# Linear attention in front of two expert layers: key/value sums, numerators and denominators issued in five bursts per unit instead of in each step

## The chip, the cores and the metric

The kernel runs on one core of a Trainium2 chip. The metric is the device time of one execution in microseconds, the median over three runs. Inputs and outputs lie in device memory; the clock runs from the first instruction to the last, with the launch around it.

## The reference

Only the first third of the reference, linear attention, is touched by the change. Per batch and head (8 x 8, 576 tokens, head size 64):

```python
def phi(x):                                # 64 -> 128 -> 256 features
    proj = np.einsum('bhsd,df->bhsf', x, w_phi)
    proj = proj - np.max(np.abs(proj), axis=-1, keepdims=True)
    return np.concatenate([np.exp(proj), np.exp(-proj)], axis=-1)
q_p, k_p = (phi(q), phi(k))
kv = np.einsum('bhsf,bhsd->bhfd', k_p, v)
z = np.sum(k_p, axis=2)
num = np.einsum('bhsf,bhfd->bhsd', q_p, kv)
den = np.einsum('bhsf,bhf->bhs', q_p, z)[..., None] + 1e-06
out = num / den
```

Its output goes through a top-1 mixture of 8 experts (512 -> 1024 -> 512) and then through a dense layer with a softmax gate, a norm and a second matrix. Those two layers, the last two thirds of the time, are not edited.

## The kernel before, in words

**Units and steps.** Attention is cut into 8 units: a pair of batches (`p2`) by a group of four heads (`g`). A unit is 9 key jobs k0 to k8 and 9 query jobs q0 to q8. Jobs 0 to 3 belong to the first batch of the pair (half 0), 5 to 8 to the second (half 1), and job 4 holds the last 64 tokens of both. The main loop (L682) runs over 72 steps `st`, one k and one q job each; in the last unit the keys come first.

One step issues, in this order on TensorE (PE), which executes the order as written:

- `s0` for the *next* step (L255): four 128-wide transposes of loaded k and q, which ScalarE (ACT) and VectorE (DVE) split into `hi` and `lo`;
- twice: `proj` (L267 to L269), six matmuls against `w_phi` into a PSUM tile `mm` (four buffers). DVE then takes a maximum (L271) and subtracts it (L273); ACT exponentiates keys into `e` (L277, L278). Behind each `proj` come `q_features` (L330) of the job two steps back, and some small finishing pieces ("f" items: transposes L399, L416, L545, L560);
- `accum_kv` (L283) for the key job of two steps back. It is eight matmul instructions on 64 columns of the array (two instructions run side by side), called here a kv series; jobs 4 and 5 have a series that uses only 64 rows as well (called rest). GpSimd (POOL) adds the same `e` into `es` (L322, L298), which later gives z;
- up to two "64" items: numerators, `num_part` (L440), on 64 columns like kv;
- up to one "32" item: `z_sum` (L384) or `den_part` (L454), on 32 columns, four instructions side by side.

So the array is used in three widths in each step: 128, then 64, then 32 columns. Below, "step i" is the step whose kv series belongs to key job k_i, which is `st` = 9 x unit + i + 2.

`finish_kv` (L468) makes the items of a half after job 4 or job 8: one `z_sum` that may run from the next step, four `num_part` (two token ranges `CHUNKS` of 256 and 320 columns by two head pairs) and two `den_part`, each behind the pieces that it needs (`kf_part` for numerators, `z_part` behind `z_sum` for denominators). When all are done the finishing chain starts (division on DVE; in units with g = 1 also the gating of the expert layer).

**Loads.** SyncE (SP) issues the loads of k, q and v in its own order. `unit(ui + 1)` (L696) asks for the next unit at step 2. The step numbered i = 6 begins with the transposes of job 0 of the next unit, so it needs the next unit's data first of all. The order of DVE, ACT, POOL and SP is made by the framework's planner.

Of the kernel before, what the change touches and what calls it, by code (L numbers as in the profile page):

```python
# [8 lines left out]
F32 = mybir.dt.float32  # L9
# [8 lines left out]
P = 128  # L18
B, H, S, D, F = 8, 8, 576, 64, 128
# [16 lines left out]
YCOLS = PAD + NTOK  # L36
LAG = 8
LAGF = 2
FSLOT = (1, 2)
COLS64 = 2  # L40
COLS32 = 1
TAIL = 1
BIAS = 8
BGN = 1
# [149 lines left out]
def attention(ctx, tc, c, cnt, xe, q, k, v, ld, early, m, late):  # L194
# [3 lines left out]
    w3p = ctx.enter_context(tc.tile_pool(name="a_w3", bufs=3))  # L198
# [63 lines left out]
    def proj(hl, a, kind):  # L262
        hi, lo = hl
        pj = mmp.tile([P, 4, F], F32, name="mm")
        for j in range(2):
            o = pj[:, 2 * j : 2 * j + 2, :].rearrange("p a f -> p (a f)")
            T.matmul(o, lhsT=hi[:, 2 * a + j, :], rhs=c.wphi_hi, start=(j == 0), stop=False, skip_group_check=True)  # L267
            T.matmul(o, lhsT=hi[:, 2 * a + j, :], rhs=c.wphi_lo, start=False, stop=False, skip_group_check=True)
            T.matmul(o, lhsT=lo[:, 2 * a + j, :], rhs=c.wphi_hi, start=False, stop=True, skip_group_check=True)  # L269
        m = w3p.tile([P, 4], F32, name="m")  # L270
        V.tensor_reduce(out=m, in_=pj, axis=AX.X, op=ALU.max, apply_absolute_value=True)  # L271
        x = w3p.tile([P, 4, F], F32, name="xs" + kind, bufs=4 if kind == "q" else 3)
        V.tensor_tensor(out=x, in0=pj, in1=m.unsqueeze(2).broadcast_to([P, 4, F]), op=ALU.subtract)  # L273
        if kind == "q":
            return x
        e = w3p.tile([P, 4, 2, F], F32, name="e", bufs=4)
        A.activation(e[:, :, 0, :], x, AF.Exp)  # L277
        A.activation(e[:, :, 1, :], x, AF.Exp, scale=-1.0)  # L278
        return e
# [78 lines left out]
    def run_items(kind, count):  # L358
        ran = 0
        while ran < count:  # L360
            it = next((x for x in items if x.kind == kind and x.runnable()), None)
            if it is None:
                break
            if isinstance(it, Chain):
                said = next(it.gen, items)
                if said is not items:
                    if said:
                        until = step[0] + said[1]
                        it.kind, it.ready = said[0], lambda: step[0] >= until
                    ran += 1  # L370
                    continue
            else:
                it.fn()
            it.done = True
            items.remove(it)
            ran += 1
        return ran
# [3 lines left out]
    def z_sum(u, half):  # L381
        zp = mmp.tile([P, 2 * F], F32, name="mm")
        for h in range(4):
            T.matmul(  # L384
                zp[32 * h : 32 * h + 32, :], lhsT=c.ones32, rhs=u.es[half][:, h, :, :],
                start=True, stop=True, tile_position=(0, 32 * h), skip_group_check=True,
            )
        zs = w2p.tile([P, 2, F], F32, name="zs")
        A.copy(zs, zp.rearrange("p (a f) -> p a f", a=2))
        u.zs[half] = zs  # L390

    def kf_part(u, half, j):
        if j == 0:
            u.kf[half] = w2p.tile([P, 2, 4, D], F32, name="kf")
        kf = u.kf[half]
        gdt = gd[(2 * u.g + half) % 2]
        tp = tps.tile([P, 2, P + 2 * E], F32, name="tp")
        for fh in range(2):
            T.matmul(  # L399
                tp[:, fh, :], lhsT=u.kt[half][:, j, fh * F : (fh + 1) * F], rhs=c.idwg[:, 2 * u.g + j, :],  # L400
                start=(fh == 0), stop=True, skip_group_check=True,
            )
        A.copy(
            kf[:, :, 2 * j : 2 * j + 2, :],
            tp[:, :, 0:P].rearrange("p a (h d) -> p a h d", h=2),
        )
        A.copy(
            gdt[:, :, 2 * j : 2 * j + 2, 0:E],
            tp[:, :, P : P + 2 * E].rearrange("p a (h e) -> p a h e", h=2),
        )  # L410

    def z_part(u, half):
        gdt = gd[(2 * u.g + half) % 2]
        tp = tps.tile([P, 2, P], F32, name="tp")
        for fh in range(2):
            T.transpose(tp[:, fh, :], u.zs[half][:, fh, :], c.ident)  # L416
        A.copy(gdt[:, :, :, E : E + 1], tp.rearrange("p a (h n) -> p a h n", n=32)[:, :, :, 0:1])
# [43 lines left out]
    def outputs(u, half):  # L461
        u.num[half] = w1p.tile([P, 2, 4 * P], F32, name=f"num{half}")
        u.den[half] = w1p.tile([P, 4 * P], F32, name=f"den{half}")
        if half == 0:
            u.num[2] = w1p.tile([P, 2, P], F32, name="num2")
            u.den[2] = w1p.tile([P, P], F32, name="den2")

    def finish_kv(u, half):  # L468
        at = step[0]
        zi = Item("32", lambda: z_sum(u, half), ready=lambda: step[0] > at)  # L470
        kfs = [Item("f", lambda j=j: kf_part(u, half, j)) for j in range(2)]
        zt = Item("f", lambda: z_part(u, half), after=[zi])
        begin = Item("0", lambda: outputs(u, half))
        parts = []
        for ci, (_, need) in enumerate(CHUNKS[half]):
            ok = lambda need=need: u.qdone.issuperset(need)
            for j in range(2):
                parts.append(Item("64", lambda ci=ci, j=j: num_part(u, half, ci, j), after=[begin, kfs[j]], ready=ok))
            parts.append(Item("32", lambda ci=ci: den_part(u, half, ci), after=[begin, zt, *kfs], ready=ok))

        def rest():
            yield from finish(u, half, 0, 4)
            if half == 1:
                yield from finish(u, 2, 0, 1)
            if u.g == 1:
                yield "0", 0
                yield from gating(u, 4 * half, 4 + half)
                if u.p2 == 2 and half == 1:
                    early.pick(cnt[0])
                    early.ready = True  # L490

        Chain("f", rest(), after=parts)
# [148 lines left out]
    def unit(ui):  # L641
        if ui not in U and ui < len(units):
            U[ui] = load_unit(*units[ui])
        return U.get(ui)
# [21 lines left out]
    def last_unit():  # L666
        return U.get(len(units) - 1)
# [10 lines left out]
    n = len(steps)  # L678
    feats = {}
    bias = late()  # L680
    tail = []
    for st in range(n + LAGF):  # L682
        step[0] = st
        if st == 9 * 7 + PRE:
            assert early.ready
            m.prefetch()
        if st == 9 * 7 + STEP0:
            for i in range(RING0):
                m.split_raw(1, i)
        if st == BIAS:  # L690
            bias()
        run_items("0", 4)
        if st + 1 < n:
            ui, jobs = steps[st + 1]
            if ("k", 5) in jobs:
                unit(ui + 1)  # L696
            hl[st + 1] = s0(unit(ui), jobs)
        old = feats.pop(st - LAGF, ())
        u_old = unit(steps[st - LAGF][0]) if st >= LAGF else None
        kjobs = [(i, x) for kind, i, x in old if kind == "k"]  # L700
        qjobs = [(i, x) for kind, i, x in old if kind == "q"]
        if st < n:
            h_ = hl.pop(st)
            feats[st] = []
        for a in range(2):
            if st < n:
                kind, i = steps[st][1][a]
                feats[st].append((kind, i, proj(h_, a, kind)))
            if qjobs:
                i, x = qjobs.pop(0)  # L710
                q_features(u_old, i, x)
                u_old.qdone.add(i)
            run_items("f", FSLOT[a])
        for i, x in kjobs:
            accum_kv(u_old, i, x)
            if i in (4, 8):
                if i == 8 and u_old is last_unit():
                    tail.append(finish_last(u_old))
                else:
                    finish_kv(u_old, i // 5)  # L720
        run_items("0", 4)
        run_items("64", COLS64)
        run_items("32", COLS32)
        if st >= n and tail:
            for _ in range(TAIL):
                next(tail[0], None)
# [806 lines left out]
```

## Time and profile before

| | us |
|---|---|
| median of 3 runs | 1337.44 (1335.55 to 1338.93) |
| the profiled execution | 1330.52 |
| its span, first to last instruction | 1328.8 |
| attention, to the last key/query matmuls | about 437 of it |

The profiled execution is 6.9 us below the median; sums are made against it. In views by time, "start" is microseconds from the first instruction. A PE duration holds the way through the array, so what a matmul costs in a full queue is read from the start of one to the start of the next. The timeline merges neighbours of one kind into one line with a count.

### The profile page before, as it was taken

Reading aid. Unit: us, or ns where it says so; the run is one execution under the profiler, and the core shown is the slowest. Engines: PE = TensorE matmul, PEld = TensorE weight load, DVE = VectorE, ACT = ScalarE, POOL = GpSimd, SP = SyncE. Lnnn points to the kernel's source line nnn. Section 1 sums busy time; section 2 is a strip of 40 time slices with the busy share of each in tenths; the row PEclk is TensorE's granted clock in tenths of the full one; section 3 lists DMA queues with packets and bytes.
Section 4 is the critical chain, followed back from the end, with each engine's and each line's share of the span. In section 5 each row is a group of like instructions: output and inputs, shape, how many; then the busy total and the mean of one; then the engine's idle time right before and its main releaser. Section 6 shows DMA issues by size and latency. Waiting matters only on the chain.

```text
span 1328.8 us, 25500 instructions
## 1 busy us (share of the span) xinstructions
PE 1298.4 (98%) x9522; PEld 1092.2 (82%) x9522; DVE 811.5 (61%) x1571; ACT 668.1 (50%) x1254; POOL 433.8 (33%) x493
## 2 busy tenths in 40 slices
PE   8999999999999989999999999999999999999997
PEld 7677777777775889999999999898987777888885
DVE  8758867866885748888888654444433334444442
ACT  6666666666664345555565554444433333443332
POOL 7555665674672200000000322232312232322331
PEclk9999999999999989999999999999999999999998
DMA  8712421341142132224432211124435542111110
GB/s 239 208 52 63 133 94 56 98 136 49 50 134 76 67 95 80 74 71 142 145 80 81 65 41 56 41 61 146 127 81 159 159 145 70 49 40 48 40 41 24
DMA packets 123119, 120.08 MB, mean 90 GB/s; under 512 B 35664, under 2 KB 109552, under 8 KB 122992
## 3 DMA queue, kind: packets, MB, share of 16 engines
q1 hardware_dynamic: 117008, 99.30, 25.6%
q0 software_dynamic: 5824, 19.04, 3.9%
q8 instruction: 77, 1.26, 0.4%
q14 instruction: 50, 0.41, 0.1%
q10 hardware_dynamic: 160, 0.07, 0.0%
HBM read 148.32 MB, written 33.02 MB: 136 GB/s over the span
## 4 chain that ended last, share of the span: by engine, by line
PE 63%; issue 1%; ACT 0%; POOL 0%; POOLq 0%
PE tp L1074 43%; PE h L1074 15%; PE tp L1098 2%; PE tp L898 1%; PE tp L1349 1%; PE tp L1333 1%; PE tp L1280 0%; POOLq L1529 0%; ACT sq L1253 0%; ACT lnTh L887 0%; PE tp L1109 0%; ACT wab L1268 0%; POOL rs L1258 0%; PE tp L1162 0%; POOL rs L1256 0%
## 5 line engine op out<-in xcount | busy, mean ns | idle before, releaser
L322 POOL TENSOR_TENSOR es<-es,e 128x512 f32<-128x512 f32 x128 | 163.6, 1285 | 103.9 <-ACT e L278 92.3
L1074 PE MATMUL tp<-xTh,whi 128*128 128x256 f32 x432 | 122.5, 284 | 2.9 <-PEq L1412 2.9
L1233 DVE TENSOR_REDUCE s_mx<-h 128x1 f32<-128x512 f32 x72 | 46.4, 686 | 125.4 <-PE h L1074 125.4
L1074 PE MATMUL tp<-xTh,wlo 128*128 128x256 f32 x432 | 121.5, 281 | 1.2 <-DVE wlo L926 1.2
L1074 PE MATMUL tp<-xTl,whi 128*128 128x256 f32 x432 | 121.3, 281 | 0.0
L1074 PE MATMUL tp<-hTl,whi 128*128 128x256 f32 x432 | 120.9, 280 | 0.0
L1074 PE MATMUL tp<-hTh,wlo 128*128 128x256 f32 x432 | 120.8, 280 | 0.0
L1074 PE MATMUL tp<-hTh,whi 128*128 128x256 f32 x432 | 120.7, 280 | 0.0
L926 POOL TENSOR_TENSOR wlo<-ldk,whi 128x1024 fp32r<-128x1024 f32 x6 | 14.6, 2435 | 314.8 <-PE tp L1074 296.0
L1269 POOL DMA_INDIRECT out_dram<-wab,gt x36 | 38.5, 1070 | 222.5 <-ACT wab L1268 221.8
L1238 ACT ACTIVATE ex<-h,s_mx,gt 128x1024 f32<-128x1024 f32 x36 | 43.4, 1206 | 134.2 <-DVE s_mx L1235 70.6
L271 DVE TENSOR_REDUCE m<-mm 128x4 f32<-128x512 f32 x144 | 97.1, 680 | 16.0 <-PE mm L269 15.9
L259 DVE TENSOR_TENSOR lo<-tp,hi 128x512 fp32r<-128x512 f32 x72 | 49.5, 688 | 84.0 <-ACT hi L258 83.5
L267 PE MATMUL mm<-wphi_hi,hi 128*128 128x256 f32 x288 | 93.5, 325 | 1.0 <-ACT hi L258 1.0
L1074 PEld LDWEIGHTS tp<-xTh,whi 128*128 128x128 f32 x432 | 82.0, 190 | 3.3 <-issue 3.1
L888 DVE TENSOR_TENSOR lnTl<-tp,lnTh 128x512 fp32r<-128x512 f32 x74 | 47.6, 685 | 58.4 <-ACT lnTh L887 58.4
L1074 PEld LDWEIGHTS tp<-xTh,wlo 128*128 128x128 f32 x432 | 82.0, 190 | 1.5 <-DVE wlo L926 1.5
L338 ACT ACTIVATE qp<-tp 128x512 f32<-128x512 f32 x128 | 69.4, 597 | 26.1 <-PE tp L330 23.2
L1074 PEld LDWEIGHTS tp<-xTl,whi 128*128 128x128 f32 x432 | 82.0, 190 | 0.2
L1074 PEld LDWEIGHTS tp<-hTh,whi 128*128 128x128 f32 x432 | 81.5, 189 | 0.4
L1074 PEld LDWEIGHTS tp<-hTl,whi 128*128 128x128 f32 x432 | 81.5, 189 | 0.3 <-DVE hTl L1089 0.2
L1074 PEld LDWEIGHTS tp<-hTh,wlo 128*128 128x128 f32 x432 | 81.5, 189 | 0.2
(427 smaller groups left out, 3928.2 us busy)
## 6 DMA issues: line engine op xcount, KB each, us to landing
ldk<-in_moe_w_dram SPq DMA_DIRECT2D x66, 512.0 KB
ldv<-in_moe_w_dram SPq DMA_DIRECT2D x66, 512.0 KB
ldq<-in_moe_w_dram SPq DMA_DIRECT2D x44, 512.0 KB
yd<-yo SPq DMA_DIRECT2D x36, 256.0 KB
yin<-yd SPq DMA_DIRECT2D x18, 512.0 KB
xin<-xe SPq DMA_DIRECT2D x16, 512.0 KB
ldk<-in_k_dram SPq DMA_DIRECT2D x15, 512.0 KB
ldq<-in_q_dram SPq DMA_DIRECT2D x15, 512.0 KB
```

Source lines behind the costliest of these rows:

```text
L259: V.tensor_tensor(out=lo, in0=tp, in1=hi.bitcast(F32), op=ALU.subtract)
L267: T.matmul(o, lhsT=hi[:, 2 * a + j, :], rhs=c.wphi_hi, start=(j == 0), stop=False, skip_group_check=True)
L271: V.tensor_reduce(out=m, in_=pj, axis=AX.X, op=ALU.max, apply_absolute_value=True)
L322: G.tensor_tensor(out=eo, in0=eo, in1=ev[:, :, r, :], op=ALU.add)
L338: A.activation(u.qp[half][:, fh, 2 * hp : 2 * hp + 2, o : o + 2 * P], tp.rearrange("p (h r) t -> p h (r t)", r=2), AF.Exp, scale=sc,)
L888: self.tc.nc.vector.tensor_tensor(out=lo, in0=tp, in1=hi.bitcast(F32), op=ALU.subtract)
L926: eng.tensor_tensor(out=lo, in0=src, in1=hi.bitcast(F32), op=ALU.subtract)
L1074: T.matmul(o, lhsT=l, rhs=r, start=first and n == 0, stop=last and n == 2, skip_group_check=True)
L1098: T.transpose(tp[:, j, :], src[:, (b0 + j) * P : (b0 + j + 1) * P], c.ident)
L1233: V.tensor_reduce(out=mx, in_=h[:, sl], axis=AX.X, op=ALU.max, negate=True)
L1238: A.activation(ex, h, AF.Exp, bias=mx, scale=g, accum_out=sm)
L1269: ins = G.indirect_dma_start(out=out, out_offset=bass.IndirectOffsetOnAxis(ap=ys.pop(i)[2].bitcast(I32), axis=0), in_=ob, in_offset=None,)
```

## The change

Key jobs are not accumulated in their step. They are put into a list `held`, and the list is worked off in steps where the current key job is 1, 2, 4, 6 or 8 (`FLUSH`). "64" and "32" items run only in these steps too, until the last six steps of the loop, and up to two "32" items run instead of one. The tile `e` gets a fifth buffer, since it is kept longer.

```diff
+LAST = 6
 COLS64 = 2
-COLS32 = 1
+COLS32 = 2
+FLUSH = (1, 2, 4, 6, 8)
...
-        e = w3p.tile([P, 4, 2, F], F32, name="e", bufs=4)
+        e = w3p.tile([P, 4, 2, F], F32, name="e", bufs=5)
...
-    tail = []
+    tail, held = [], []
...
-        for i, x in kjobs:
+        held += [(u_old, i, x) for i, x in kjobs]
+        flush = any(i in FLUSH for i, x in kjobs)
+        for u_old, i, x in held if flush else ():
             accum_kv(u_old, i, x)
             if i in (4, 8):
                 if i == 8 and u_old is last_unit():
                     tail.append(finish_last(u_old))
                 else:
                     finish_kv(u_old, i // 5)
+        if flush:
+            held = []
         run_items("0", 4)
-        run_items("64", COLS64)
-        run_items("32", COLS32)
+        if flush or st >= n - LAST:
+            run_items("64", COLS64)
+            run_items("32", COLS32)
```

## Rows read from the trace of the kernel before

**Rows 1.** Page, part 1: busy time, share of span, instructions of each engine.

```profile
PE 1298.4 (98%) x9522; PEld 1092.2 (82%) x9522; DVE 811.5 (61%) x1571; ACT 668.1 (50%) x1254; POOL 433.8 (33%) x493
```

**Rows 2.** Windows; stretch, length, busy of PE, PEld, DVE, ACT, POOL, clock, DMA, GB/s.

```profile
23.27:26.70 3.43, 3.43 (x30) 2.77 (x29) 3.43 (x7) 2.70 (x6) 2.57 (x2) 1.00 1.06 374
...
300.00:350.00 50.00, 49.64 (x442) 35.82 (x440) 39.92 (x83) 33.14 (x80) 29.77 (x26) 1.00 0.21 65
```

**Rows 3.** Waits of PE, 30 to 400 us: total us, times, longest.

```profile
PE tp L560 <- DVE lo L259: 1.9, 6, 0.3
```

**Rows 4.** Timeline of PE: start, us, line, tiles; a kv series alone in its step.

```profile
104.35 0.60 PE L330 MATMUL tp<-ident,xsq 128*128 128x128 f32 x4
104.79 0.60 PE L545 MATMUL tp<-ident,den 128*128 128x128 f32 x4
...
105.81 0.28 PE L269 MATMUL mm<-wphi_hi,lo 128*128 128x256 f32 x1
106.02 1.08 PE L283 MATMUL kv<-e,ldv 128*64 128x256 f32 x8
107.04 0.44 PE L255 MATMUL tp<-ident,ldk 128*128 128x128 f32 x2
107.31 0.38 PE L255 MATMUL tp<-ident,ldq 128*128 128x128 f32 x2
```

**Rows 5.** Timeline of PE: rest, kv, numerators and z in one step; two kv series.

```profile
86.88 1.08 PE L283 MATMUL kv<-e,ldrv 64*64 64x256 f32 x8
87.89 1.08 PE L283 MATMUL kv<-e,ldv 128*64 128x256 f32 x8
88.81 2.11 PE L440 MATMUL mm<-qp,kf 128*64 128x256 f32 x16
90.85 0.64 PE L384 MATMUL mm<-es,ones 128*32 128x256 f32 x8
91.42 0.44 PE L255 MATMUL tp<-ident,ldk 128*128 128x128 f32 x2
...
399.14 1.95 PE L283 MATMUL kv<-e,ldv 128*64 128x256 f32 x16
400.92 2.11 PE L440 MATMUL mm<-qp,kf 128*64 128x256 f32 x16
```

**Rows 6.** Timeline of PE: denominators, behind numerators and behind a kv series.

```profile
46.14 1.07 PE L454 MATMUL mm<-qp,gd 128*32 128x256 f32 x16
47.14 0.44 PE L255 MATMUL tp<-ident,ldk 128*128 128x128 f32 x2
...
49.56 1.08 PE L283 MATMUL kv<-e,ldv 128*64 128x256 f32 x8
50.57 1.28 PE L454 MATMUL mm<-qp,gd 128*32 128x320 f32 x16
```

**Rows 7.** Timeline of SP's queue: issue of a load of unit 1.

```profile
33.00 0.51 SPq L228 DMA_DIRECT2D ldq<-in_q_dram  x1
```

**Rows 8.** Timeline of PE, unit 0, steps 5 and 6: starts, and idle time with releaser.

```profile
33.62 1.08 PE L283 MATMUL kv<-e,ldrv 64*64 64x256 f32 x8
...
38.86 0.41 PE L255 MATMUL tp<-ident,ldk 128*128 128x128 f32 x2 [0.25 <-DMA ldk<-in_k_dram]
40.53 0.44 PE L255 MATMUL tp<-ident,ldq 128*128 128x128 f32 x2 [1.26 <-DMA ldq<-in_q_dram]
```

**Rows 9.** Windows: a stretch in which PE waited, and the granted clock behind it.

```profile
465.00:468.00 3.00, 0.40 (x4) 0.43 (x5) 0.20 (x1) 1.28 (x2) 0.00 (x0) 1.00 0.22 67
468.00:470.00 2.00, 2.00 (x15) 2.00 (x13) 2.00 (x2) 2.00 (x3) 0.00 (x0) 0.66 0.01 4
470.00:472.00 2.00, 2.00 (x11) 2.00 (x10) 1.99 (x4) 1.71 (x4) 0.00 (x0) 0.50 0.00 0
```

**Rows 10.** Timeline of DVE: the first and the last of one step's five operations.

```profile
277.07 0.69 DVE L259 TENSOR_TENSOR lo<-tp,hi 128x512 fp32r<-128x512 f32 x1 [4.68 <-ACT hi L258]
...
279.47 0.68 DVE L273 TENSOR_TENSOR xsq<-mm,m 128x512 f32<-128x512 f32 x1
```

## The prediction

> **What bounds the kernel now.** I read the page first, for the engine that is never idle, then windows over attention, then the waits of PE, and last PE's timeline step by step. PE is busy 98% of the span [rows 1], and in a stretch of attention 49.64 of 50 us, with DVE at 39.92, ACT at 33.14 and POOL at 29.77 [rows 2]. PE hardly waits there: the largest wait on another engine between 30 and 400 us is 1.9 us in all [rows 3]. So in the edited stage nearly every nanosecond that leaves PE's queue leaves the time, and every one that PE must wait for comes on top. A busy PE can still hold avoidable time, so the next thing to look at is start to start.
>
> **The price of a change of array width.** A kv series alone in its step: the last projection matmul starts at 105.81 and the series at 106.02, 0.21 us later, where neighbouring projections lie 0.115 apart. (That is an estimate: a plain step takes 3.43 us [rows 2]; less 0.21, the series' 1.02, the 0.05 below and eight transposes at 0.11, 1.27 is left for eleven.) So 0.095 is lost going in. The series takes 1.02 to the start of the next transposes, whose first two take 0.27 where four L330 transposes take 0.44, so 0.22 for two: 0.05 lost coming out [rows 4]. Together 0.095 + 1.02 + 0.05 = 1.165 us. A kv series followed by other 64-wide work takes 0.92 (87.89 to 88.81), and two in a row 1.78 (399.14 to 400.92), so the second costs 0.86 [rows 5]. A series put beside another thus saves 1.165 - 0.86 = 0.30 us. Rest followed by kv takes 1.01 instead of 0.86 [rows 5]: 0.15 for going from 64 rows to 128, so where kv3 is put in front of rest of job 4, the saving is 0.30 - 0.15 = 0.15.
>
> A 32-wide series: behind kv it delays the next start from 0.92 to 1.01, so 0.09 to enter [rows 5, 6]. z, eight instructions of 256 columns, takes 0.57 [rows 5], sixteen of denominators take 1.00 [rows 6]; eight more cost 0.43, so 0.57 - 0.43 = 0.14 is fixed. The way back to 128 that a 64-wide series would need anyway is 1.02 - 0.92 = 0.10 [rows 4, 5]. One 32-wide series fewer saves 0.09 + 0.14 - 0.10 = 0.13.
>
> **How many.** By the rule of `FLUSH`, kv0 joins kv1, kv3 joins rest 4, kv5 joins kv6, kv7 joins kv8. In the last unit the last two pairs are already one step each. Following the items: before, a half has its z, its first and its second denominator in three steps; after, half 1 has z in step 1 and both denominators in step 2, half 0 has z in step 6 and both in step 8. That is one 32-wide series fewer per half. Units 1 to 7 save 7 of kv0, 6 of kv5 and 6 of kv7, 19 x 0.30 = 5.7; 7 of kv3, 7 x 0.15 = 1.05; and 32-wide series, 7 second halves (unit 0's lies in unit 1) and 6 first halves, 13 x 0.13 = 1.7. Sum 8.45 us. Unit 0 is counted apart.
>
> **What unit 0 pays.** Step 6 of unit 0 begins with the transposes of unit 1's k and q. The load of q is issued by SP at 33.00 [rows 7], in SP's own order, and PE waits for them already: its k transposes start at 38.86 after 0.25 idle, the q transposes at 40.53 after 1.26 [rows 8]. Before, the 5.2 us in front of that are filled from 33.62 on with rest, kv5, two numerators and z [rows 8]. After the change step 5 is no flush step: all of this is moved behind the transposes. PE arrives at 33.62 - 0.095 - 0.30 (kv0) - 0.15 (kv3) = 33.1 and waits for k until 38.86 and q until 40.53. What was done in that wait is now done after 40.53: rest 1.01, kv5 0.86, two numerators of 256 columns 2 x 0.86 (they have a kv series' shape), z 0.43, together 4.0 us; kv7 joining kv8 gives 0.30 back, and the number of 32-wide series after 40.53 stays two. Net +3.7 us. The bounds: 0, if the data were there at 33 (nothing in rows 7 and 8 says so), and 5.2, if all of the stretch came back. I take 3.7.
>
> **The clock behind that wait.** At 465 PE was busy for 0.40 of 3 us, and behind it the granted clock was 0.66 and then 0.50 for 2 us each [rows 9]: the lower level of 1.2 GHz beside 2.4. What that cost is 2 x 0.34 + 2 x 0.50 = 1.7 us of PE time. The gap in unit 0 will be longer, 5.7 us and then 1.3, and what follows is PE-bound. The bounds are 0 (behind the 1.26 us gap before, nothing falls) and twice 1.7, if the clock needs longer; I take 1.7, the row nearest to it. The Trainium skill, "TensorE: Matmul & The Clock Gate", section "HAM oscillation — how this bites in real kernels", states that a PE left waiting between bursts falls to half rate and starts the next burst cold; rows 9 agree, and by that rule the term stands, while without it the sum would be 1.7 us lower.
>
> **DVE in the light steps.** A plain step with kv takes PE 3.43 [rows 2], one without kv 3.43 - 1.165 = 2.27. DVE needs five operations per step, 0.60 us apart (277.07 to 279.47 is four of them), 3.0 us [rows 10]. So the light steps without other PE work (3 and 7; steps 0 and 5 carry more transposes) give DVE 0.73 us more than PE leaves it. What hides this: the steps around are heavy, four `mm` buffers let PE run two steps of projections ahead, and `lo` is made a step ahead. Where the cover is thin is step 4, whose L560 transposes wait for a `tp` buffer behind `lo` already (0.3 us each, 1.9 in all [rows 3]). Bounds: -1.9 if those waits go, and 13 light steps (6 units of two, one in the last) x 0.73 = +9.5 if nothing hides it. I take +1.0, nearest to the waits seen.
>
> POOL's sums depend on `e` and not on the kv series, and the fifth `e` buffer keeps the distance between last use and rewriting at a step; v tiles are freed a step later at most, with their next loads not needed for several steps: both at 0. ACT evacuates up to four results in a burst, at about a third to a half of PE's time for them: 0.
>
> **Sum.** -8.45 + 3.7 + 1.7 + 1.0 = -2.05 us, from 1330.52 to 1328.5 in a profiled execution. The median before lies 6.9 above that execution; from it, 1337.44 - 2.05 = 1335.4.
>
> **The rivals.**
> 1. *The gain comes through whole.* If unit 1's data come in time (SP's order is made anew and could bring the loads forward) neither the 3.7 nor the 1.7 is paid, and unit 0 adds 3 x 0.30 + 0.15 + 0.13 = 1.2 of its own: -8.45 - 1.2 + 1.0 = -8.65, 1328.8 us. For it: the loads need nothing from PE. Against it: nothing in the edit touches them, and PE waited for them before [rows 8].
> 2. *DVE takes PE's place in the light steps.* Place: steps 3 and 7 of each unit, at the transposes that need `tp` and the projections that need `lo`. Price: up to 9.5 us instead of 1.0, so -8.45 + 3.7 + 1.7 + 9.5 = +6.45, 1343.9 us. It makes the kernel slower as soon as it takes more than 3.05 us, a third of the full price. For it: DVE at 3.43 of 3.43 us in a step of unit 0 [rows 2]. Against it: over 50 us DVE has 10 us free [rows 2].
> 3. *The change does not save what it says:* the 0.30 is no cost of changing width but of these instructions wherever they stand. Then nothing is saved, and 3.7 + 0.3 + 1.7 remain: +5.7, 1343.1 us. Against it: two series in a row took 1.78 and not 2.33 [rows 5].
>
> **How the numbers follow.** Forecast 55%, with its own range from -4.75 (no lower clock, no DVE waits) to +1.5 and 1.5 of scatter of the three runs: 1331 to 1340. Rival 1 20%, rival 2 17%, rival 3 8%. 0.3%, 4.0 us, is about what a measurement of this kernel can tell from no change. Faster by more: rival 1 and a tenth of the forecast's share and some more, 28%. Slower by more: most of rivals 2 and 3, 18%. Within: 54%. The range is 1328.5 to 1342.
>
> **What would show it.** Right: pairs of kv series of 1.8 us and no kv between projections in steps 0, 3, 5, 7; one PE wait of 5 to 6 us for unit 1's k near 33 us and one for q until about 40.5; a clock of 0.5 behind it; from 100 to 350 us a unit shorter by about 1.3 us, with waits of PE on DVE below half a microsecond. Wrong: L255 in unit 0 not waiting longer than before (rival 1); PE waits on `lo` or L273 in most light steps (rival 2); the time from 100 to 350 us unchanged (rival 3).

## The result, and the profile after

The changed kernel takes 1343.9 us (median of 5 runs, 1343.18 to 1345.53), beside 1337.44 before: ratio 1.0054, 95% interval 1.0042 to 1.0067. It is slower. The forecast was 1335.4 with a range to 1342.0, so the time lies outside, on the side and nearly at the number of rival 2.

The profiled execution takes 1343.83 us, its span 1342.1. All of the difference to the span before, 13.3 us, lies in attention: the first matmul of the expert layers (L660, L658 before) starts at 443.69 instead of 430.42. That is twice the difference of the medians, because the profile before lacks stops that other executions of the same kernel have; the first experiment shows them.

Page, part 1, after. PE's busy time falls by 1.9 us [rows 1] while the span grows:

```profile
PE 1296.5 (97%) x9522; PEld 1100.2 (82%) x9522; DVE 804.5 (60%) x1571; ACT 665.6 (50%) x1254; POOL 435.2 (32%) x493
```

Timeline of PE in unit 1, steps 8 and 0 (start, us, line, tiles):

```profile
103.62 1.95 PE L285 MATMUL kv<-e,ldv 128*64 128x256 f32 x16
105.39 2.32 PE L442 MATMUL mm<-qp,kf 128*64 128x320 f32 x16
107.65 2.15 PE L456 MATMUL mm<-qp,gd 128*32 128x256 f32 x32
109.73 0.44 PE L257 MATMUL tp<-ident,ldk 128*128 128x128 f32 x2
```

Two kv series take 1.77 us from start to start (105.39 - 103.62), both denominators 2.08. So the change does what it says, at the price that was worked out from [rows 4 to 6]. What it adds is in the waits of PE, 30 to 400 us (total us, times, longest), which answer to [rows 3]:

```profile
PE tp L257 <- issue: 4.4, 2, 2.2
PE tp L562 <- DVE gs L553: 3.2, 6, 0.5
PE tp L562 <- DVE lo L261: 3.2, 6, 0.8
PE tp L257 <- ACT gd L409: 2.9, 1, 2.9
PE tp L401 <- DVE lo L261: 2.3, 4, 1.0
PE tp L257 <- ACT e L280: 1.9, 1, 1.9
```

Before, the longest single wait on another engine in this stretch was 0.7 us. To see where the waits fall, cut attention at the transposes of step 0 (first L255 or L257 of the step, from PE's timeline). The last column is the changed kernel again (experiment `e5_after_again`, below), on a chip where the kernel before takes 1329 us. A unit from 2 on that kept the stops of the kernel before and had the forecast's saving of a full unit, 1.31, would take 51.76 - 1.31 = 50.45 us.

| us | before | after | after, again |
|---|---|---|---|
| start to step 0 of unit 1 | 55.67 | 58.93 | 61.43 |
| unit 1 | 51.37 | 50.80 | 50.80 |
| units 2, 4, 6, mean | 51.77 | 52.75 | 52.75 |
| units 3, 5, mean | 51.75 | 54.07 | 50.82 |
| unit 7 and on, to L660 | 64.58 | 67.59 | 68.92 |
| sum | 430.42 | 443.69 | 441.05 |

Units 3 and 5 differ, 54.81 and 53.33. Three places cost time: unit 0, the even units, and step 0 of units 3, 5 and 7. Each is read by itself.

**Unit 0.** PE's timeline, answering to [rows 8], and the windows behind it (clock in the third column from the end):

```profile
37.55 0.41 PE L257 MATMUL tp<-ident,ldk 128*128 128x128 f32 x2 [1.89 <-ACT e L280]
38.93 0.44 PE L257 MATMUL tp<-ident,ldq 128*128 128x128 f32 x2 [0.98 <-DMA ldq<-in_q_dram]
42.39 1.39 PE L285 MATMUL kv<-e,ldrv 64*64 64x256 f32 x8
```

```profile
39.00:40.00 1.00, 1.00 (x8) 1.00 (x9) 0.71 (x2) 0.54 (x1) 1.00 (x1) 0.82 1.27 257
40.00:43.00 3.00, 3.00 (x16) 2.58 (x17) 1.79 (x3) 1.14 (x3) 0.25 (x1) 0.50 1.19 248
43.00:44.00 1.00, 1.00 (x12) 0.46 (x10) 1.00 (x3) 0.12 (x1) 0.00 (x0) 0.97 0.85 287
```

The series of rest and kv stand behind the transposes, PE stops in front of them, and the clock falls to its lower level for 3 us: 0.18 + 3 x 0.50 + 0.03 = 1.7 us lost. In `e5_after_again` PE stops there for 2.09 and 0.96 us, and the lower level lasts three times as long (windows):

```profile
38.00:41.00 3.00, 2.43 (x12) 2.43 (x13) 2.47 (x4) 0.59 (x1) 2.50 (x2) 0.50 1.23 286
41.00:44.00 3.00, 3.00 (x16) 2.13 (x14) 2.16 (x5) 1.09 (x2) 0.00 (x0) 0.50 1.10 324
44.00:47.00 3.00, 3.00 (x16) 1.48 (x14) 0.59 (x1) 1.15 (x2) 1.61 (x2) 0.50 1.14 301
47.00:50.00 3.00, 3.00 (x26) 1.64 (x26) 0.00 (x0) 0.43 (x2) 0.93 (x1) 0.83 1.14 322
```

With 0.1 before 38 us that is 0.1 + 3 x 1.5 + 0.5 = 5.1 us of clock, of the 5.76 us that unit 0 takes longer there than before. The clock falls at later stops too: to 0.50 for 3.4 us near 169 and near 384 us in the profile after, and for 6.8 us from 379 us on in `e5_after_again`, each behind the stop in step 0 of unit 3 or 7.

**Even units, steps 3 to 5.** Windows by step, unit 2, of the changed kernel (length, then busy time of PE, PEld, DVE, ACT, POOL):

```profile
122.01:129.48 7.47, 7.47 (x82) 5.09 (x78) 3.18 (x5) 4.38 (x12) 3.07 (x3) 1.00 0.01 2
129.48:132.39 2.91, 2.91 (x30) 2.90 (x27) 1.52 (x3) 2.04 (x5) 2.71 (x2) 1.00 0.00 0
132.39:138.82 6.43, 5.59 (x48) 4.12 (x46) 6.43 (x19) 3.99 (x11) 2.69 (x3) 1.00 0.01 3
138.82:143.25 4.43, 3.49 (x29) 3.08 (x27) 4.43 (x14) 2.26 (x4) 3.72 (x4) 1.00 0.74 218
```

Step 2 is heavy now: PE works 7.47 us on it, over half of that on numerators and denominators, which give VectorE nothing to do at once, and VectorE is busy for 3.18 of them. Step 3 takes PE 2.91 us, and what it makes piles up: in steps 4 and 5 VectorE is busy for 6.43 of 6.43 and 4.43 of 4.43 us (its five operations per step, the finishing of half 1 and the gating of the unit before), and PE waits three times:

```profile
134.96 0.66 PE L562 MATMUL tp<-ident,num 128*128 128x128 f32 x4 [0.84 <-DVE lo L261]
141.14 0.41 PE L562 MATMUL tp<-ident,num 128*128 128x128 f32 x2 [0.54 <-DVE gs L553]
142.65 0.51 PE L401 MATMUL tp<-idwg,kt 128*128 128x144 f32 x2 [0.41 <-DVE lo L261]
```

In the kernel before, the same three steps take 3.87, 4.51 and 8.20 us, and VectorE is nearly as full, but PE's kv series lies beside it in each (windows of the kernel before, unit 2):

```profile
126.49:130.36 3.87, 3.87 (x37) 3.22 (x33) 3.87 (x7) 2.45 (x5) 3.78 (x2) 1.00 0.00 0
130.36:134.87 4.51, 4.51 (x40) 3.73 (x38) 4.12 (x9) 3.68 (x9) 3.32 (x4) 1.00 0.70 221
134.87:143.07 8.20, 7.88 (x69) 5.23 (x67) 8.05 (x19) 4.79 (x13) 7.62 (x9) 1.00 0.71 218
```

**Step 0 of units 3, 5, 7.** Timeline of all engines in unit 3 after the change (its own first profile):

```profile
165.24 1.49 PE L401 MATMUL tp<-idwg,kt 128*128 128x144 f32 x8
165.91 0.96 POOL L630 DMA_INDIRECT xe<-xt,g_dsti  x1 [0.30 <-issue]
...
167.18 0.96 POOL L630 DMA_INDIRECT xe<-xt,g_dsti  x1 [0.30 <-issue]
...
168.41 0.37 ACT L405 COPY kf<-tp 128x256 f32<-128x256 f32 x1 [2.49 <-remote]
168.68 0.19 ACT L409 COPY gd<-tp 128x32 f32<-128x32 f32 x1
168.92 0.44 PE L257 MATMUL tp<-ident,ldrk 128*128 128x128 f32 x2 [2.19 <-issue]
```

PE starts the eight L401 transposes at 165.24; ScalarE, idle, takes the first four only at 168.41, and PE's next transposes wait for that buffer. Nothing in the profile is late but the signal itself. In between GpSimd issues the scatter (L630). The same place in `e5_after_again`:

```profile
167.77 1.14 PE L401 MATMUL tp<-idwg,kt 128*128 128x144 f32 x8
...
168.44 0.96 POOL L630 DMA_INDIRECT xe<-xt,g_dsti  x1 [0.30 <-issue]
168.46 0.37 ACT L405 COPY kf<-tp 128x256 f32<-128x256 f32 x1 [0.55 <-PE tp L401]
...
168.97 0.44 PE L257 MATMUL tp<-ident,ldrk 128*128 128x128 f32 x2
```

There the copy follows after 0.69 us instead of 3.17, with the scatter in the same place, and PE does not wait. By the semaphore events of the traces, worked out matmul by matmul, a completion normally comes 0.29 us after the start; beside the scatter up to 2.8 us here and 4.2 us in unit 7.

### The profile page after: what moved, and what is told of

The parts are those of the page before. It is cut to its first block, busy times and chain, and to the rows that moved or that the text cites. A ratio compares the mean times of both kernels' runs of the same rounds, so it can differ in the third digit from the quotient of the medians.

```text
span 1342.1 us, 25488 instructions
## 1 busy us (share of the span) xinstructions
PE 1296.5 (97%) x9522; PEld 1100.2 (82%) x9522; DVE 804.5 (60%) x1571; ACT 665.6 (50%) x1254; POOL 435.2 (32%) x493
## 4 chain that ended last, share of the span: by engine, by line
PE 62%; issue 1%; DVE 0%; ACT 0%; POOL 0%; POOLq 0%; DVEq 0%
PE tp L1081 42%; PE h L1081 15%; PE tp L1105 2%; PE tp L905 1%; PE tp L1356 1%; PE tp L1340 1%; PE tp L1287 0%; POOLq L1536 0%; DVE wlo L933 0%; DVE hTl L1096 0%; ACT sq L1260 0%; ACT lnTh L894 0%; PE tp L1116 0%; ACT wab L1275 0%; POOL rs L1265 0%
## 5 line engine op out<-in xcount | busy, mean ns | idle before, releaser
L270 PE MATMUL mm<-wphi_lo,hi 128*128 128x256 f32 x288 | 82.1, 285 | 0.0
L271 PE MATMUL mm<-wphi_hi,lo 128*128 128x256 f32 x288 | 82.0, 285 | 0.0
```

## The experiments

Each time is a median beside runs of the kernel before on the same chip. Those came to 1329 us on two chips and to 1335 on three. Each chip was used in one session, so a property of a chip is not told apart from one of the hour, and the chip of the first result is not on record.

**1. The kernel before, again** (no edit).

> The kernel before, once more, for a second trace: its first profiled execution was 6.9 us below its median. Theory A (the change saves array-width changes but adds three kinds of stop: unit 0's wait for loads, PE waits on DVE in steps 4 and 5, PE stops in step 0 of units 3, 5 and 7): 1337 us, and a trace without a PE stop above 1.5 us between 50 and 400 us. Rival B (such stops come and go in any execution and are no part of the change): the trace of an execution near 1337 us has stops of 2 us in the 50 to 400 us as well, some 7 us in all.

1335.66 us, ratio 1.0003 [0.9993, 1.0012], span 1334.0. In this trace completions of matmuls come late beside the scatter at six places of attention, the worst of each place 1.9 to 3.45 us after the start, where the one in [rows 1 to 10] has none over 0.5. Waits of PE, 30 to 400 us:

```profile
PE tp L560 <- DVE lo L259: 5.9, 6, 1.7
PE tp L399 <- DVE xt L562: 1.0, 2, 0.5
```

The units with these places take 0.75 to 1.34 us longer, 6.8 in all, while PE has kv series, numerators and z to go on with in steps 8 and 0 of the kernel before; unit 0 is 1.3 us shorter here. These 5.5 us make the 5.2 between the two profiled executions up to 0.3, nearer to rival B than to theory A. That the rest of the 6.9 us between the first profile and its median is of the same kind is likely and not shown.

**2. Unit 0 left as it was, and two more on top of it.**

```diff
-        flush = any(i in FLUSH for i, x in kjobs)
+        flush = st < 11 or any(i in FLUSH for i, x in kjobs)
```

> The changed kernel, but every step up to st = 10 (unit 0's key jobs) is a flush step, as before the change. Theory A: the wait for unit 1's keys and queries is filled again and the clock does not fall there, about 5 us faster than the changed kernel, 1339 us, with steps from unit 1 on unchanged. Rival B (loads set the pace of the start either way): no gain, 1344 us.

1339.57 us, ratio 1.0031 [1.0019, 1.0044]: unit 0 is worth 0.23% or 3.1 us. Step 0 of unit 1 starts at 55.2, and the clock near 40 us stays up. The stops in step 0 of units 3, 5, 7 stay and in this profile even grow (L257 behind `gd`, 8.1 us in three); the profiled execution, 1344.30, is the slowest of the nine.

With `FLUSH = (1, 2, 3, 4, 6, 8)` as well:

> The kernel of e2 with step 3 a flush step in every unit, so that steps 3 and 4 are as before the change. Theory A: PE's wait on lo at the L562 transposes of step 4 (0.84 us in units 2, 4 and 6, about 1.0 us of time with what follows) goes, at 0.15 us more per unit for a change of array width: 1 to 2 us faster than e2, 1337.5 us. Rival (the wait comes from the planner's order on DVE in these units, not from the light step in front): as slow as e2 or 1 us slower.

1339.42, ratio 1.0025 [1.0013, 1.0036]: not to be told from the one before, where 1 to 2 us less were expected. Step 3 has its kv series again, and the wait of step 4 falls only from 0.84 to 0.56 us in unit 2, while step 5 has a wait on `lo` of 1.60; the even units take 53.03 us, not less. So holding kv3 is not all that makes the even units long.

With the last pause of the gating two steps longer in units of the first two pairs (`yield "0", (3 if u.p2 < 2 else 1)`), to move the scatter:

> The kernel of e2 with the last piece of the gating (ranks, and POOL's scatter of the tokens) two steps later in the first two batch pairs, so that in units 3 and 5 it falls behind step 0; unit 7 is left as it was. Theory A (PE is held up while POOL issues the scatter beside a step of small pieces): no PE stop of 2 to 3 us in step 0 of units 3 and 5, that of unit 7 stays; 2 x 2.7 and one fall of the clock, 1.7, less: about 7 us faster than e2, 1332 us. Rival (the stop belongs to step 0's own pieces, two L401 groups back to back in front of the next transposes): all three stops stay, 1339 us.

1340.74, ratio 1.0035 [1.0022, 1.0047]. The scatter did not move: its first issue behind unit 2 is at 158.44 instead of 156.74, and unit 1 starts 1.7 us later too, so it is at the same place beside step 0. The run tests nothing.

**3. One step held at a time.** The changed kernel, with all steps in `FLUSH` but one. `COLS32 = 2` and the fifth `e` buffer stay, and what they do alone was not run, so a gain or a loss below is that of the held step together with them:

```diff
-FLUSH = (1, 2, 4, 6, 8)
+FLUSH = (0, 1, 2, 3, 4, 5, 6, 8)      # step 7 held; likewise without 3, 5, 0
```

> The changed kernel, but only step 7 is held (kv7 into step 8, no numerators or denominators in step 7); all other steps are flush steps. Before measures 1335.1 us in these rounds. Theory C (kv, numerators and denominators are the only PE work of a step that needs no fresh result of ACT or DVE; they cover PE's waits, and it is the places where cover is taken from that cost): step 7 has no wait to cover, so the array-width saving comes through, 6 or 7 units x (0.30 + 0.13) = 2.8 us, 1332.3 us, ratio 0.998. Rival D (collecting costs about the same in every place, a quarter of the 7 us each): 1337 us, ratio 1.0013.

1333.01, ratio 0.9985 [0.9975, 0.9995].

> Only step 3 is held (kv3 in front of rest in step 4). Theory C: saves 0.15 in each of 8 units, 1.2 us, and brings the wait of PE on lo in step 4 from 0.3 to 0.84 us in units 2, 4 and 6, and 0.2 in the others: some 2 to 3 us; sum +1 to +2, 1336.5 us, ratio 1.001. Rival D: 1337 us.

1346.09, ratio 1.0079 [1.0066, 1.0092]: the costliest step of all, missed by both.

> Only step 5 is held (rest, kv5, two numerators and z of a half into step 6). Theory C: unit 0 loses the cover of its wait for unit 1's loads, 3.7 to 5.4 us with the clock, the first half's scatter in units 2, 4 and 6 finds PE uncovered in step 5 instead of 6, and 7 x 0.30 = 2.1 is saved: +3, 1338 us, ratio 1.0022. Rival D: 1337 us.

1339.65, ratio 1.0026 [1.0015, 1.0036].

> Only step 0 is held (kv0 and the second half's z into step 1). Theory C: in units 3, 5 and 7 the second half's scatter meets a step 0 of small dependent pieces, PE stands for 2.7 us or more each and the clock falls for 3.4 us behind it, 3 x (2.7 + 1.7) = 13 us less what those places cost before (0.7 to 1.2 each, 3 us) less 7 x 0.43 = 3.0: +7, 1342 us, ratio 1.005. Rival D: 1337 us.

1333.26, ratio 0.9984 [0.9974, 0.9993]: a step that the theory held for costly gains.

Hold 3 in windows by step, unit 2 (steps 2, 3, 4), and its waits of PE, 30 to 400 us:

```profile
123.42:127.30 3.88, 3.88 (x37) 3.22 (x33) 2.52 (x6) 2.45 (x5) 2.96 (x4) 1.00 0.35 137
127.30:131.64 4.34, 3.66 (x31) 3.25 (x30) 3.53 (x8) 2.88 (x7) 3.69 (x5) 1.00 0.32 123
131.64:137.25 5.61, 4.94 (x38) 3.47 (x38) 5.61 (x13) 3.54 (x9) 5.38 (x4) 1.00 0.00 0
```

```profile
PE tp L562 <- DVE lo L261: 7.3, 11, 1.2
PE tp L401 <- DVE lo L261: 3.3, 3, 1.2
PE tp L257 <- DVE xt L564: 2.2, 6, 0.4
```

Step 3 carries the finishing transposes L562, whose results VectorE takes. Without kv 3, PE has 3.66 us of work in a step that takes 4.34, and in step 4 VectorE is full, 5.61 of 5.61. Steps 3 and 4, between which kv 3 is only moved, take 4.34 + 5.61 = 9.95 us instead of 3.87 + 4.51 = 8.38. It is the mechanism of the even units, and it appears with a single step held; more waits on `lo` stand in steps 5 and 8 (1.17 and 1.21 us), and unit 6 alone takes 59.23 us, of which unit 7 gives back a part (61.86 instead of 65.72 in experiment 1).

**4. VectorE made lighter.** The maximum is taken over half of the features (which leaves the other half out):

```diff
-        V.tensor_reduce(out=m, in_=pj, axis=AX.X, ...
+        V.tensor_reduce(out=m, in_=pj[:, :, 0 : F // 2], axis=AX.X, ...
```

> Left out here and in the next two kernels: the maximum over the 128 features is taken over the first 64 alone, so one of VectorE's five operations per projection pair, twice a step, falls from 0.68 to about 0.35 us; the output differs. This one is the kernel before with that edit, and the base for the other two. Theory V (VectorE is the bound of PE in steps 3 to 5, and the work that needs no fresh result covers it in the kernel before): PE's waits on lo fall from 5.9 us to under 3, time 1331 to 1335. Rival P (the stops come from PE's late completion signals beside GpSimd's scatter, VectorE has room): waits on lo stay at 4 to 6 us, time 1334 to 1336.

1333.66 beside 1329.07: slower, ratio 1.0031 [1.0019, 1.0042], which no theory expected. VectorE has its operations in another order, and in unit 2 two small ones fall beside GpSimd's additions (timeline of both engines):

```profile
123.51 4.83 POOL L298 TENSOR_TENSOR es<-es,e 64x1024 f32<-64x1024 f32 x2 [5.47 <-ACT e L278]
...
123.57 2.36 DVE L621 TENSOR_TENSOR g_rkb<-g_rk,g_base 128x32 f32<-128x32 f32 x1
...
125.96 2.42 DVE L622 TENSOR_TENSOR g_rkb<-g_rkb,g_oh 128x32 f32<-128x32 f32 x1
```

In the kernel before the same two operations take 0.18 and 0.19 us. Here each ends with one of the two additions of 2.42 us, and `lo` waits behind them: 53.25 us for unit 2 instead of 51.77.

> Hold step 3 alone, with the maximum over half of the features. Holding step 3 alone cost 10.7 us over before. Theory V: with 0.66 us a step less on VectorE, the loss against the kernel before with the same edit goes to 0 to +4 us (1332 to 1338), and waits on lo between 30 and 460 us fall from 11.3 us (8.0 and 3.3) to under 5. Rival P: the loss stays at 8 to 11 us, 1342 to 1346, with the waits in place.

1340.14, so 6.5 us over the kernel before with the same edit, instead of 10.7: between the two theories. Units 2 and 3 together take 105.75 us, 0.6 more than there (105.12), where holding step 3 had cost 2.6 us beside experiment 1 (108.20 and 105.60); most of the rest lies at the end of unit 6, in a stop of 3.8 us. But the base has the two long operations just shown: beside the unedited kernel before, whose units 2 and 3 take 103.52 us in [rows 1 to 10]'s profile, it is still 2.2 us. So the comparison speaks for VectorE only weakly.

> The changed kernel with the maximum over half of the features. Theory V for the even units (2.2 us each in steps 4 and 5 by VectorE) and P for step 0 of units 3, 5, 7 (2.7 us each and the clock behind two of them): the waits of steps 4 and 5 shrink, about 5 us gained, and the stops in step 0 stay at over 1.5 us; 1336 to 1339. V alone for both: under 1334. P alone: 1342 to 1344.

1331.98: 1.7 us under the kernel before with the same edit. On this chip no trace shows late completions, and the changed kernel itself did not run on it, so this run alone can't tell how much VectorE gave back.

> Only steps 0 and 7 held, each of which gained about 2 us alone (1333.3 and 1333.0 beside 1335.4). If the steps are independent: 1331.0, ratio 0.997. If held steps disturb each other, since with the series of steps 7 and 0 both away the late completions of step 8 and 0 have less left to hide behind: 1334 to 1337, and a stop of over 1.5 us at the transposes of step 0 in units 3, 5, 7.

1334.62 beside 1329.07, ratio 1.0043 [1.0031, 1.0055]: the two steps that gained alone lose together. But they gained on a chip with late completions, and this one has none; alone they did not run here. In this trace the waits that grew are those on `lo` (L562 4.4, L401 4.2 us) and one of 2.4 us on ScalarE at L418 in unit 7.

**5. The changed kernel again, and three more.**

> The changed kernel, unchanged. If the chip shows late completions (before at about 1335): 1341 to 1345, stops of over 2 us at the transposes of step 0 in units 3, 5, 7. If it does not (before at about 1329): theory V, VectorE crowded in the light steps, expects the even units' waits on lo and gs to stay and the step 0 stops to go, 1333 to 1337, still slower than before; rival P, all of it from late completions, expects 1326 to 1329, faster or equal.

1338.92 beside 1328.98, ratio 1.0071 [1.0059, 1.0083]. In attention no completion comes more than 0.7 us after its start, the stops in step 0 of units 3 and 5 are gone, and the kernel is still 9.9 us slower. So late completions are not needed for the loss. The even units take what they took in the first profile after the change (52.75). What stops PE in step 0 of unit 7 here is seen in the timeline:

```profile
374.90 1.14 PE L401 MATMUL tp<-idwg,kt 128*128 128x144 f32 x8
...
379.08 1.04 ACT L932 CAST w<-ldk 128x1024 fp32r<-128x1024 f32 x1 [4.04 <-DMA ldk<-in_moe_w_dram]
380.03 0.37 ACT L405 COPY kf<-tp 128x256 f32<-128x256 f32 x1
...
380.54 0.69 PE L257 MATMUL tp<-ident,ldrk 128*128 128x128 f32 x2 [4.49 <-ACT gd L409]
```

ScalarE's queue has a cast of a prefetched expert weight in front of the copy of `kf`; the cast waits 4.04 us for its load, and PE, with nothing held back for it, waits 4.49. Behind the stop the clock is at 0.50 (windows):

```profile
381.00:384.00 3.00, 3.00 (x16) 3.00 (x15) 2.02 (x4) 1.55 (x6) 2.31 (x2) 0.50 1.06 394
```

With 0.68 in the 3 us on either side that is 3.4 us of clock. Of the 10.6 us by which L660 comes later here than in the profile before (441.05 and 430.42), unit 0 makes 5.8, unit 7 4.3 and units 1 to 6 0.5; 8.5 of it is lower clock, less a little that passed while PE stood still.

> The changed kernel with the maximum over the first 64 of 128 features (left out: the other 64), as in a_half_max, now on one chip with the changed kernel. V: 4 us or more faster than the changed kernel. P: within 2 us of it.

1332.26, 6.7 us under the changed kernel, as the theory of a crowded VectorE had it. The units show that little of this came from where it said. Of 8.5 us between the two profiles (L660 at 432.51 and 441.05), units 1 to 6 give 2.3, unit 0 2.2 and unit 7 4.0, the last two with 5.1 us less of lower clock. All of the 2.3 is in the odd units (50.01 to 50.03 us, so that they save 1.4 and 1.7 beside the kernel before, no less than the widths' 1.31). The even units take 52.79 us, no less than the 52.75 without the edit: step 5 is 0.8 us shorter, but in step 1 a wait on `lo` grew from 0.21 to 1.14 us. There two of the gating's VectorE operations of 32 columns (L578, L581) take 0.82 and 0.89 us beside two additions by GpSimd, and `lo` is queued behind them. So in the even units, where most of the loss lies, the test does not settle what VectorE's work is worth.

Finishing pieces kept out of the light steps, up to two behind each projection elsewhere:

```diff
-            run_items("f", FSLOT[a])
+            if not any(x in (3, 5, 7) for x, _ in kjobs_) or st >= 9 * 6 or st < 11:
+                run_items("f", FSLOT[a])
```

> The changed kernel, with the small finishing pieces (transposes of numerators and denominators, whose results VectorE takes) kept out of the light steps 3, 5 and 7, up to two behind each projection in the other steps. V: VectorE has its five operations alone in a light step, waits on lo and gs in steps 3 to 5 halve, 3 to 6 us faster than the changed kernel. P: no gain, within 2 us. Against V speaks that the pieces then crowd the heavy steps, and that the gating and its scatter come later: if that decides, slower than the changed kernel.

1345.46, 6.5 us slower than the changed kernel: the case against. Waits on `gs` are gone and those of L562 on `lo` down to 0.6 us, but L562 waits on ScalarE (5.9 us, 8 times) and L271 on `lo` (4.9, 5 times) in the heavy steps.

More scatters in the kernel before, where it has none:

```diff
+            if i == 5 and u_old.g == 1 and st < 9 * 6:
+                ...
+                for a in range(4):
+                    ins = nc.gpsimd.indirect_dma_start(out=xe2[0], ..., in_=ef[:, 0:ROW], ...)
```

> The kernel before, with four more scatters by GpSimd, of 128 rows each into a buffer that nothing reads, behind key job 5 in units 1, 3 and 5, where it has none. P, on a chip with late completions: completions of PE up to 1 us or more late in step 5 or 6 of these three units, as beside the scatter of the even units, and up to 1.4 us lost in each, 2 to 5 us in all; on a chip without, 0 to 1 us. V: no late completions there, and 0 to 1 us on either.

1330.02, ratio 1.0008 [0.9999, 1.0017]. This chip shows no late completions beside any scatter, so the run says what four more scatters cost there (nothing that can be told from zero), not whether scatters make completions late.

**6. The cast out of ScalarE's queue, and the odd units alone.**

```diff
-        self.split(self.raw[i], hi, lo, ...)
+        if self.nsplit == 1:
+            g.tensor_copy(hi, self.raw[i])            # g: GpSimd
+            g.tensor_tensor(out=lo, in0=self.raw[i], in1=hi.bitcast(F32), op=ALU.subtract)
+        else:
+            self.split(self.raw[i], hi, lo, ...)
```

> The changed kernel, with the first split of an expert weight (cast and subtraction, L932 and L933) made by GpSimd instead of ScalarE and VectorE. If the cast that waits for its load in ScalarE's queue makes the stop at step 0 of unit 7, the stop of 3 to 4.5 us goes and the lower clock behind it too: 1332 to 1336 on a chip where the kernel before takes 1329, 1337 to 1341 where it takes 1335. Rival: the stop belongs to the gating chain or to late completions, and stays over 2.5 us: 1337 to 1341, and 1342 to 1345.

1344.06 beside 1334.86, ratio 1.0054 [1.0040, 1.0067]: no gain, and the stop stays. This chip has late completions, and they make the stop without the cast:

```profile
382.44 0.76 PE L401 MATMUL tp<-idwg,kt 128*128 128x144 f32 x4 [0.93 <-ACT qp L340]
...
385.00 0.37 ACT L405 COPY kf<-tp 128x256 f32<-128x256 f32 x1 [2.62 <-remote]
...
385.52 0.44 PE L257 MATMUL tp<-ident,ldrk 128*128 128x128 f32 x2 [2.32 <-ACT gd L409]
```

Whether it would have gone on a chip without them is not shown.

Only units 1, 3, 5, 7 collected, with the same split (`flush = u_old is None or u_old.g == 0 or ...`):

> As x4, and the series are collected in units 1, 3, 5 and 7 only; units 0, 2, 4 and 6 issue them in each step as before. Theory V with the account by units: unit 0 costs nothing, the even units take 52.0 us as before, the odd ones 50.8 instead of 51.5, so up to 3 us less than the kernel before: 1326 to 1329 where that takes 1329, 1331 to 1335 where it takes 1335. Rival: the even units' time was not made by their own held steps but by the order that the planner makes for VectorE, ScalarE and GpSimd over all units, and stays at 52.5 us or more: not faster than before, 1330 to 1335 where that takes 1329.

1338.2 beside 1334.86, ratio 1.0024 [1.0015, 1.0033]. The rival was right: the gain of the odd units does not come by itself. The even units, which hold nothing here but get a part of the odd units' finishing, take 56.4 to 56.5 us with waits on `lo` of up to 1.74; units 3 and 4 together take 106.76 where they took 105.61 in experiment 1. Only holding step 0 or step 7 alone beat the kernel before, by 0.15%, on the one chip that they ran on, which has late completions.

## Why the prediction was wrong

- **Bound and price of width: right for a pair.** Two kv series were put at 1.78 and take 1.77. The saving of a full unit, 1.31, is seen whole only with VectorE lighter (experiment 5, odd units); otherwise unit 1 went from 51.37 to 50.80 and units 3 and 5, without late completions, from 51.75 to 50.82.
- **Unit 0: near in its sum by luck, wrong in its terms.** 3.7 for the loads and 1.7 for the clock make 5.4. Measured against the profile before were 3.26 in the changed kernel's profile and 5.76 in `e5_after_again` (the kernel before itself takes 54.34 to 55.67 to this point in three profiles), and 3.1 by the ratio of experiment 2. The wait for the loads was put at 5.7 and 1.3 us and came to 1.89 (which the profile puts down to ScalarE) and 0.98, and 2.09 and 0.96: the loads came 1.3 to 2.0 us earlier than in [rows 8], and PE arrived at 35.7 and 35.1, not at 33.1. The clock cost 1.7 us, as in [rows 9], in the first and 5.1 in the second. So of the 3.7 there are 1.6 and 0.7.
- **DVE in the light steps: the step that failed.** It was put at +1.0, "nearest to the waits seen". Without late completions units 1 to 6 together take 0.53 us more than before, where the widths alone should have saved 6 x 1.31 = 7.9: so 8.4 us are lost there, 2.3 in each even unit (52.75 to 50.45) and 0.4 to 0.7 in each odd one. Of these, 5.8 are PE's waits on VectorE (in `e5_after_again` 3.2 on `gs`, 3.2 and 1.3 on `lo`, less 1.9 before [rows 3]); the other 2.6 stand in no wait that the profile names. The upper bound was 9.5. The place was in part right (L562 behind `lo` in step 4, but also step 5, and nothing in step 7), the weight wrong for two reasons. VectorE's room was read as a mean over 50 us, 39.92 busy [rows 2], though the even units' steps 3 to 5 run at 16.04 of 16.58 us before the change. And "the steps around are heavy" was taken for cover; it is the opposite: the collected work makes nothing for VectorE at once, which is busy for only 3.18 of the 7.47 us of step 2 and is late in the steps behind. That PE waits there on a full VectorE is shown, with step 3 held alone as well; that the held series are the whole cause is argued, since the even units got no shorter where kv3 was back in its step (53.03, experiment 2), where VectorE's work was lighter (52.79, experiment 5) or where they held nothing (experiment 6).
- **Rival 2's number came out by chance.** With its whole price it gave 1343.9, the time measured. Its 9.5 us were to lie in the light steps 3 and 7; the measured time is made of waits in steps 4 and 5 of the even units, late completions, a stop in unit 7 and the clock.
- **The clock was counted once.** Behind the stops of units 3 and 7, which the forecast did not have, it fell too: 1.7 us each in the first profile, 3.4 in unit 7 of `e5_after_again`.
- **"ACT evacuates ...: 0" failed as well,** in unit 7: a weight's cast, for which ScalarE waited 0.63 us in the kernel before, makes it wait 4.04 in `e5_after_again`, in front of the copy of `kf`, and PE stands for 4.49. No row of those read for the prediction lay there. That the cast alone makes the stop is not shown (experiment 6).
- **The time from which the sum was made.** It was carried from the profile to the median by adding 6.9 us, as if these had nothing to do with the change. Most of them are late completions, as far as experiment 1 shows, and the change takes away what covers them: units 3 and 5 take 4.0 and 2.5 us longer where they occur, the first with 1.7 us of lower clock in it.

Not explained: what makes completions late, and why on some chips only (that they come beside the scatter was seen, not tried), why unit 0's loads come at other times from run to run, and how much of each loss hangs on the order that the planner makes anew for VectorE, ScalarE and GpSimd with every edit, and what the second "32" item per step does alone. The order is no small thing: an edit that only lightens VectorE made the kernel before 4.6 us slower.

## What to carry to other kernels

Work that needs no fresh result is what an in-order engine does while the others are late; collecting it into bursts saves the changes of width and lays every lateness bare, its own neighbours' and that of a rare neighbour such as a weight's cast. Before collecting, read the busy time of the follower engines step by step and not over the stage: where one of them is full in the steps that become light, do not put its excess at little without a reason. And compare a profile with the median of its runs first: a gap of 0.5% can be the very thing that the change touches.

## What the runs showed of the hardware

- PE's completion signals came up to 2.8 us after the start of the matmul in unit 3 and 4.2 in unit 7 (profile after; `x4_split_on_pool` likewise), instead of 0.29, while GpSimd issued indirect DMAs; on three chips and in the changed kernel's first profile beside the same scatters, on two chips never, with the same kernel. The signal only is late: the next matmuls of PE's queue run on (eight L401 from 165.24 to 166.73, ScalarE's copy at 168.41).
- A VectorE operation of 32 columns with both inputs in SBUF took 2.36 us beside a GpSimd addition, and ended with it, instead of 0.18. The Trainium skill, "SBUF — State Buffer", section "SBUF: two separate sides", says that the two engines share a port pair which one of them holds for a whole instruction; the trace agrees.
- The lower clock behind a stop lasted from 3.4 us (unit 0 after the change, PE stopped for 1.89 and 0.98) to 10 us (the same place in `e5_after_again`, where PE was busy for 0.52 of the 3 us before it fell).
